# A planned TensorE order, searched on with new costs for scores, V and landings, on one Trainium2 core

## The chip, the cores and the metric

The kernel runs as one program on one core of a Trainium2 chip. The metric is the device time of that core in microseconds (us), the median of several runs. Engines are named as the profile names them: PE is TensorE's matmul and PEld its weight load, DVE is VectorE, ACT is ScalarE, POOL is GpSimd, SP is SyncE, whose queue issues most of the DMAs.

## The reference, cut to what matters

```python
# x: (1, 2048, 576) bf16; 32 heads of 128; 8 memory rows; segments of 32 rows; FFN of 4608
def _A_ref(x, mem0, Wq, Wk, Wv, Wo, seg_len):
    ...
    for s in range(n_seg):                       # 64 segments, one after the other
        h = concatenate([mem, x[segment s]])     # 8 + 32 rows
        q, k, v = h @ Wq, h @ Wk, h @ Wv         # per head
        scores = (q @ k.T) * Dh ** -0.5          # masked with -1e9
        o = softmax(scores) @ v @ Wo
        mem = o[:, :M]                           # the next segment's memory
        outs.append(o[:, M:])
def _B_ref(x, w1, w3, w2):
    return (silu(x @ w1) * (x @ w3)) @ w2
x = x + _A_ref(_layernorm(x), ...)
x = x + _B_ref(_layernorm(x), ...)
x = x + _A_ref(_layernorm(x), ...)               # the same weights
x = x + _B_ref(_layernorm(x), ...)
```

Each layer of attention is a recurrence over 64 segments: a segment's memory rows come out of the segment before.

## The kernel before, in words

The two layers run interleaved, the second LAG = 8 segments behind the first, so a *step* t does segment t of the first layer and segment t - 8 of the second. There are 72 steps; in the first eight and the last eight only one layer is at work (40 columns a product instead of 80). The FFN works on groups of four segments (128 rows), so four steps make a period.

`make_nodes` lists the work as nodes: an engine, a planned duration, dependencies, buffers that it takes (`acq`) and frees (`rel`), and a function that emits the instructions. `plan` turns them into one order for each engine. TensorE's order is not chosen there: it is written out as strings of letters, FIRST (773 nodes), FOUR (208 nodes, a period of four steps, taken eleven times: the *rounds*) and LAST (664 nodes). For the other engines `plan` takes, among the nodes that are ready first by its own costs, the one with the lowest `prio`, so their order, the choice of ACT or VectorE for nodes of kind "AD", the buffer numbers and the order of SP's DMAs follow from the planned costs and from TensorE's letters. The emitter then records the instructions in that order, and each engine runs its own in line.

The letters that the prediction speaks of: Q and q are the products for query and key of four heads (32, and 8 of the weights' last 64 rows); S the scores of a group of eight heads; T transposes of the probabilities on TensorE, in steps of one layer (32 groups in FIRST, 32 in LAST); P the product of the transposed probabilities with V; O and o the output projection (32 and 8); V, v, X, x and G, g the products for V; F and f the FFN's first matmuls for 256 hidden columns, W and w its second for the first and the second layer; a, b, n layer-norm transposes, p the transposes that bring the attention's result back to rows, m those of the memory.

In steps of both layers the probabilities PB (a head group) are transposed into PTS by a DMA that SP issues (`ptd`, L1050); the chain for one group is S on TensorE, add, maximum and subtraction on VectorE, the exponential on ACT, sum, reciprocal and PB on VectorE, the DMA transpose, P. In the plan this DMA is a node "TRD" of `TRD` us with `TRL` us until it has landed. The FFN's weights come in tiles of 256 hidden columns with two buffers each for w1/w3 ("W13": four DMAs) and w2 ("W2l"), all on SP's queue.

The planned costs: `MORE` adds a time by engine and node name, and a change of TensorE's tile form adds SWITCH:

```python
        dur += MORE.get(e, {}).get(n.name, 0.0)
        if e == "PE":
            at += 1
            if not any(m in mode for m in n.mode):
                dur += SWITCH
                settle()
                mode = n.mode
            mode = [m for m in mode if m in n.mode]
```

A node of mode "full/col" can be emitted whole (128 columns of weights) or as two halves of 64 columns; `settle` gives it the form of its neighbours. "row" products work on 64 rows. The emitter's `qk`, when a pair's Q comes ahead of its q in step 0 and the pair is the first or fifth, puts twelve products on the identity in front of it:

```python
            for c in range(4 if first and t == 0 and u % 4 == 0 else 0):
                for _ in range(3):
                    self.mm(self.bk(b[1])[:], self.T.ident[:, 0:P], self.T.W[:, 4 + c, u * 512:(u + 1) * 512], True, True)
```

All matmuls stand under one line of the emitter (L627), all of ACT under L630, all of VectorE under L633, SP's loads under L636.

Of the kernel before, what the change touches and what calls it, by code (L numbers as in the profile page):

```python
# [32 lines left out]
LATS = {"PE": 0.205, "ACT": 0.165, "DVE": 0.14, "POOL": 0.04}  # L33
MORE = {"ACT": {"VMe": 0.13, "VXe": 0.13, "VGe": 0.13, "Yodd": 0.145, "PTe": 0.03, "Fwr": 0.1, "QKe": 0.02, "exp": 0.03},
        "DVE": {"VMe": 0.2, "VXe": 0.2, "VGe": 0.2, "mul": 0.07, "sum": 0.05, "add": 0.03, "POSTa": 0.12, "Fnorm": 0.13, "maxsub": 0.02},
        "PE": {"SC": 0.05, "WOt": 0.03, "VG": 0.03, "FFt": 0.01, "TR": 0.01, "QK": 0.007}}
NOW = 1.0e18
DMA_GROUPS = 4
TRD, TRL = 1.3, 2.3
POOLS = {"bank": 8, "qkt": 4, "sme": 2, "pb0": 1, "pb1": 1, "pts": 2, "ot": 3,  # L40
         "xr": 3, "xn": 2, "w13": 2, "w2": 2, "htt": 3}

# [157 lines left out]
def ewh(*ns):  # L200
# [2 lines left out]


FIRST = (
    "maqqQqQSqTQQQSqQqqSQTQqSXxVvPPTTOOPoPOooOoQqqqqQQSQVvSqqQQQTQSqqXTSPOPTPOOTooPoxOoQQqqqqQSQvVqSQqQQQSqqTPSTOPoOT"
    "PTOPooOoaQqqQQSQqqVvSqQQQqqqTSQPxTSOPXOToToPPOOooQqqqpQQSVvqqQQnQSFfqqQTQSPfqFSOTFPfWoTOPFTOPoofOoFfqqQQWSFQQqqf"
    "vVqQSTFqfQWQQSqfqFPFTSXfPWTOPOxoTFoPOOffooFVqqvQQWQSQqqfFQqqfFSQTWSPQqfqFQFSTOfPWoTOPFTOPfaOoooFfqqQQvqqSQQWSfVF"
    "qQqQWQTQPqSqTOPbSOxxXTXTPooPOOooQpQQqqqqQSnQSFfqFfQvqVSfFWQqqQfPSFPOOooFfPWOFPofOoFQqqfqQWQSqqqQQQSFSGfgqQQqgfFP"
    "GSWPGfggfFFGOPoOOPWOoooFFffqqQQWSqqQQFvSqfVqQQfFSWqQQqfPPSFFOOPWoOffFPoaoOoWQqqqqQQbSQQQqqSGSgqQQqgPGSOPGggGoPOO"  # L210
    "PooOoQqqqppQQQqvVSSnnQFfqqQQQfqqSFFSPfPwOOWoFPoffFOwPWOooFqqffQQwFWQQqqFSSFffqqQQQQqqwWSSgfGFPGgggGPGOoPOOPWOooo"
    "wFqfqqQQQQSffqqFFSQQwvqVWSFQqqffFQWPwSFffPOPOOowooWFPFOoafQQqqqWSQqqqQQQSwSbQqQgqGSggGPGPOGoPgOPOOooo"
)
FOUR = (
    "QqqqppQvVSQQnnQFqfqFSfqqQQFfqQSWPwPSFffOOowFPWoOPFOooFqfqfQQwQQqqgSWGSFqqfQQQPwQSWFqffqFSGgggGPGPOOwooOPWOooFFqq"
    "ffQQQQSwVvqqfFSQQqqWPFSFfqqfQQwOSWPFFoffPOOWPwOoooFfqqQQqqaSQQqWSQQqqqQQSbwSggGGPGPOggoGPOPOOooo"
)
LAST = (
    "QqqppQQSQqqqvVSQQnqqnQSFPqffQOoSPFOFPwWOFPfooOofQQQqqqfFSwWQQFfqqfFSwWqqQQSGqffgFQFPGgWSwPFggfGOOPoGowPOOooFvfqq"
    "VQQQQSWqqFSFqqffQQQQqqSPwWSFfPOOoWwFffPFPOOooowQWQfqqqFSFfqqQQQWSqqqQQSQbvVVSPwXvxPOPOoOPooOoQQppVqqqQQSqvqnQSnQ"  # L220
    "qffFFQTSqqQTPwFfSPWTOOPFffTFooOPWwOooFffqvVQWFQQqqqQSwSQQfqqFSTFfqqQQWTPwSPFOTOffoPTFoPOOWoowxvXVqqQQFSQqfqqQQSF"
    "QQqqqfQTwPSTSWOPFOffTFPToWoPOwOooFqqfvQQQSQqqfVwWSFFfQqqQTWqSPQQqTOSPbOxooTXPTwPOOooQQpqqqQSqQVvnSqqQQqQSQFfqTFP"
    "STfOPoTOwPTFPOOooofVvqqQQQqqSQQSFfqqFQQSTwqqQTFPffSPOTOwxXooPTFPOOffooFQQqqqqQSQFSfvVqqQQQTqqSQwTPfSOFPFTOwTooPf"
    "POfOooFvVQQqwQqqqSQqqQSQfFTSqQqQfPTSPOOooFTTPPfOOoopwfFFnFwffFFwffFFwwffFfFwFfFwffFfFwFfFwffFFwffFFwffFw"
)
ORDER = FIRST + FOUR * 11 + LAST

# [8 lines left out]
def make_nodes(em, nseg, pools, o=Opt, dma_bw=230e3, load_bw=400e3):  # L236
# [125 lines left out]
    def step(t):  # L362
        ls = layers_of(t)
        nl = 2 if both(t) else 1
# [16 lines left out]
        for g in range(NG):  # L381
            qs, qe = [], []
            for u in (2 * g, 2 * g + 1):
                q = Slot("qkt", users=1)
                b = banks()
                pq = t + o.qk + o.ustep * u
                m_ = node("PE", 32 * mm80, em.qk(t, u, b), deps=hx + hm[:1] + ([ld_h[u // 4]] if t == 0 else []),
                          prio=pq, mode="full", acq=[q] + b, name="QK")
                n = node("PE", 4 * mm80, em.qk_tail(t, u, b), deps=hx + hm + ([ld_h[u // 4]] if t == 0 else []), prio=pq + o.qkt, mode="row",
                         acq=[q] + b, name="QKt")  # L390
                rd += [m_, n]
                me[f"QK{u}"], me[f"QKt{u}"] = m_, n
# [7 lines left out]
            sc = node("PE", 8 * (0.0312 if nl == 2 else 0.029), em.scores(t, g, qs, s), deps=qe, prio=pf + o.sc, mode="col" if nl == 2 else "full/col", acq=[s, sme], rel=qs, name="SC")  # L400
# [24 lines left out]
            b = banks()  # L425
            ot = Slot("ot")
            pv = node("PE", 8 * mm80, em.pv(t, g, pts, b), deps=pe_ + vx_ev["VM", t, g] + vx_ev["VX", t - e, g],
                      prio=pf + o.pv, mode="full/col", acq=b + [ot], rel=[pts], name="PV")
            pvs[t, g] = pv
            if paired(t):  # L430
                vx_ev["VX", t + 1, g] = vg_out(t, g, gb, gd + [pv], 0)
            ote = [node("AD", ew(4 * c80), em.ot_ev(t, g, ab, b[ab], ot), deps=[pv], prio=pf, rel=[b[ab]], name="OTe") for ab in (0, 1)]
            wo = node("PE", 32 * mm80, em.wo(t, g, ot), deps=ote + ([ld_o[g]] if t == 0 else []), prio=t + o.wo + o.wog * g, mode="full",
                      acq=[y] if g == 0 else [], name="WO")
            wot = node("PE", 4 * mm80, em.wo_tail(t, g, ot), deps=[wo], prio=t + o.wo + o.wog * g, mode="col", rel=[ot], name="WOt")
            if g:
# [33 lines left out]
    def job(j):  # L470
# [36 lines left out]
        for at, pp in enumerate([npp - 1] + list(range(npp - 1)) if last else range(split, npp)):  # L507
# [5 lines left out]
            for pr_ in (2 * pp, 2 * pp + 1):  # L513
                prio = s0 + o.ff + (o.win if s0 + 4 < nst else o.last_win) * (2 * at + pr_ % 2) / NPR
                if stays:
                    w13, w2 = kept[pr_]
                    ld = []
                    w2s.append(w2)
                elif last:
                    w13 = w2 = None  # L520
                    ld = tail[pp]
                else:
                    keep = s0 < nst <= s0 + 4 and pp == npp - 1
                    w13, w2 = Slot("w13", users=2 + keep), Slot("w2", users=ne + keep)
                    kept[pr_] = w13, w2
                    ld = [node("DMA", kb(1152, 256) / dma_bw, em.load_w13(pr_, w13), prio=prio - 1, acq=[w13], lat=2.5, name="W13")]
                    lds.append(node("DMA", kb(256, 576) / dma_bw, em.load_w2(pr_, w2), prio=prio - 0.99, acq=[w2], lat=2.4, name="W2l"))
                    w2s.append(w2)
                b = banks()
                htt = Slot("htt", users=ne)  # L530
# [862 lines left out]
```

## Time and profile before

| | |
|---|---|
| median of 3 runs | 2644.31 us |
| lowest, highest | 2639.14, 2650.45 us |
| the profiled execution: time, span | 2638.71, 2636.9 us |
| instructions, matmuls | 134690, 60031 |
| busy: PE, DVE, ACT | 98%, 76%, 48% of the span |
| chain that ended last | PE 91%, DVE 4%, DMA 3% |
| mean granted TensorE clock | 0.996 |

The profile is of one execution. A matmul's duration in it is modelled and overlaps the next one's, so the time of a group of products is read from its start to the start of what follows; idle time in brackets names what ended it. One round of FOUR lasts a little over 152 us.

### The profile page before, as it was taken

Reading aid. Unit: us, or ns where it says so; the run is one execution under the profiler, and the core shown is the slowest. Engines: PE = TensorE matmul, PEld = TensorE weight load, DVE = VectorE, ACT = ScalarE, POOL = GpSimd, SP = SyncE. Lnnn points to the kernel's source line nnn. Section 1 sums busy time; section 2 is a strip of 40 time slices with the busy share of each in tenths; the row PEclk is TensorE's granted clock in tenths of the full one; section 3 lists DMA queues with packets and bytes.
Section 4 is the critical chain, followed back from the end, with each engine's and each line's share of the span. In section 5 each row is a group of like instructions: output and inputs, shape, how many; then the busy total and the mean of one; then the engine's idle time right before and its main releaser. Section 6 shows DMA issues by size and latency. Waiting matters only on the chain.

```text
span 2636.9 us, 134690 instructions
## 1 busy us (share of the span) xinstructions
PE 2574.1 (98%) x60031; PEld 2222.3 (84%) x60031; DVE 2004.5 (76%) x5137; ACT 1264.2 (48%) x3745; POOL 196.7 (7%) x253
## 2 busy tenths in 40 slices
PE   5999999999999999999999999999999999999998
PEld 4788888889888888888888888888888888888886
DVE  4787777887778678777877777787777777777876
ACT  2655553444445454444545444454545445454552
POOL 1100000000000010000001001000100001010000
PEclk9999999999999999999999999999999999999999
DMA  9065755575464656546454654655465464545357
GB/s 324 4 174 135 190 104 147 130 148 139 126 147 115 139 127 155 136 131 151 113 140 116 159 140 128 155 110 139 114 156 143 132 159 94 139 122 146 106 156 247
DMA packets 683207, 371.56 MB, mean 141 GB/s; under 512 B 233753, under 2 KB 672801, under 8 KB 681985
## 3 DMA queue, kind: packets, MB, share of 16 engines
q1 hardware_dynamic: 678944, 355.00, 53.2%
q8 instruction: 469, 7.68, 1.2%
q0 software_dynamic: 3024, 6.93, 0.9%
q10 hardware_dynamic: 656, 1.02, 0.2%
q14 instruction: 114, 0.93, 0.1%
HBM read 306.72 MB, written 2.36 MB: 117 GB/s over the span
## 4 chain that ended last, share of the span: by engine, by line
PE 91%; DVE 4%; DMA 3%; issue 1%; ACT 1%; ACTq 0%; DVEq 0%; SPq 0%
PE bank L627 91%; DMA PTS<-PB 2%; DVE HTT L633 1%; DVE PB L633 1%; DVE STAT L633 1%; DMA WV<-in_A_Wv_dram 0%; DVE SME L633 0%; DMA W<-in_A_Wk_dram 0%; DVE V L633 0%; DVE QKT L633 0%; DMA W2C<-in_B_w_dram 0%; DVE XR L633 0%; ACT HTT L630 0%; ACT HT L630 0%; DVE LNS L633 0%
## 5 line engine op out<-in xcount | busy, mean ns | idle before, releaser
L627 PEld LDWEIGHTS <-W 128*128 128x128 bf16 (+2 forms) x32920 | 1261.8, 101 | 119.8 <-issue 67.8
L627 PE MATMUL bank<-HT,W 128*128 128x80 bf16 (+3 forms) x23040 | 795.2, 197 | 21.3 <-ACT HT L630 8.2
L627 PE MATMUL bank<-XTB,W 128*64 128x256 bf16 (+5 forms) x9880 | 658.4, 264 | 2.1 <-issue 1.3
L630 ACT ACTIVATE QKT<-bank 128x256 bf16<-128x256 f32 (+4 forms) x1676 | 385.1, 309 | 302.9 <-PE bank L627 296.5
L627 PE MATMUL bank<-OT,WO 128*128 128x80 bf16 (+3 forms) x11520 | 411.6, 198 | 2.5 <-issue 1.9
L627 PEld LDWEIGHTS <-WO 128*128 128x128 bf16 (+1 forms) x11520 | 383.2, 102 | 29.9 <-issue 16.3
L630 ACT ACTIVATE V<-bank 64x512 bf16<-64x512 f32 (+1 forms) x603 | 338.0, 584 | 137.4 <-PE bank L627 131.4
L627 PE MATMUL bank<-WV,HT 128*32 128x512 bf16 (+4 forms) x3576 | 363.5, 384 | 0.3 <-issue 0.2
L627 PE MATMUL bank<-W2C,HTT 128*64 128x288 bf16 (+1 forms) x3440 | 323.8, 287 | 0.5 <-DMA W2C<-in_B_w_dram 0.5
L630 ACT ACTIVATE HTT<-bank 128x512 bf16<-128x512 f32 (+1 forms) x322 | 172.6, 551 | 300.1 <-PE bank L627 299.1
L633 DVE TENSOR_REDUCE STAT<-SME 104x8 f32<-104x320 f32 (+1 forms) x576 | 274.9, 477 | 28.2 <-ACT SME L630 21.2
L633 DVE TENSOR_TENSOR PB<-SME,STAT 40x128 bf16<-40x128 f32 (+4 forms) x912 | 274.8, 335 | 9.3 <-DMA PTS<-PB 0.5
L627 PEld LDWEIGHTS <-HT 128*32 128x32 bf16 (+4 forms) x3576 | 149.2, 99 | 147.7 <-issue 37.8
L633 DVE SCALAR_TENSOR_TENSOR HTT<-HTT,bank 128x512 bf16<-128x512 bf16 (+1 forms) x322 | 201.0, 624 | 94.4 <-ACT HTT L630 91.6
L627 PEld LDWEIGHTS <-HTT 128*64 128x64 bf16 (+1 forms) x3512 | 233.1, 106 | 31.2 <-DVE HTT L633 4.1
L1047 POOL MEMSET PB<- 128x1024 bf16 x142 | 135.0, 952 | 1657.0 <-DMA PTS<-PB 1114.3
L633 DVE SCALAR_TENSOR_TENSOR XR<-bank,XR 128x288 f32<-128x288 f32 x574 | 240.0, 447 | 20.3 <-PE bank L627 17.2
L630 ACT ACTIVATE OT<-bank 128x320 bf16<-128x320 f32 (+1 forms) x383 | 144.4, 404 | 214.5 <-PE bank L627 185.3
L630 ACT ACTIVATE SME<-SME 104x320 f32<-104x320 f32 (+1 forms) x288 | 135.5, 470 | 194.3 <-DVE SME L633 192.4
L633 DVE TENSOR_TENSOR HTT<-HTT,bank 128x512 bf16<-128x512 bf16 (+1 forms) x322 | 203.3, 631 | 28.5 <-PE bank L627 1.4
L633 DVE CAST V<-bank 64x512 bf16<-64x512 f32 (+1 forms) x261 | 178.9, 686 | 40.1 <-PE bank L627 34.9
L633 DVE TENSOR_TENSOR SME<-bank,maskb 104x320 f32<-104x320 f32 (+1 forms) x288 | 138.5, 482 | 53.8 <-PE bank L627 50.1
(59 smaller groups left out, 1383.5 us busy)
## 6 DMA issues: line engine op xcount, KB each, us to landing
W<-in_B_w_dram SPq DMA_DIRECT2D x608, 256.0 KB, 3.6
W2C<-in_B_w_dram SPq DMA_DIRECT2D x304, 288.0 KB, 3.4
W<-in_B_w_dram SPq DMA_DIRECT2D x608, 32.0 KB, 3.4
W<-in_B_w_dram SPq DMA_DIRECT2D x8, 1024.0 KB, 12.6
W<-in_A_Wq_dram SPq DMA_DIRECT2D x9, 512.0 KB, 9.9
WO<-in_A_Wo_dram SPq DMA_DIRECT2D x4, 1152.0 KB, 19.1
XR<-in_A_x_dram POOLq DMA_DIRECT2D x16, 288.0 KB, 3.1
WV<-in_B_w_dram SPq DMA_DIRECT2D x4, 1152.0 KB, 7.5
```

What stands on the lines that cost most here:

```text
L627: self.ch("PE", self.nc.tensor.matmul(out, lhsT=lhsT, rhs=rhs, start=start, stop=stop, skip_group_check=True, **k))
L630: self.ch("ACT", self.nc.scalar.activation(*a, **k))
L633: self.ch("DVE", getattr(self.nc.vector, fn_)(*a, **k))
L1047: return lambda n: self.ch("POOL", self.nc.gpsimd.memset(self.pbt(pb), 0.0))
```

## The change

Four planned costs of scores and V change: the extra for "SC" on TensorE (0.05 to 0), for "VG" (0.03 to 0.003), for "WOt" (0.03 to 0.022), and the score product itself (0.0312 to 0.0305 with both layers, 0.029 to 0.038 with one). The time to landing becomes 0.2 us shorter for the transposed P and for both kinds of FFN weights. The letters of FIRST, FOUR and LAST are the result of a search that went on from the old ones with these costs. Each string has the same letters as before, in another order; the instructions and data are otherwise the same.

```diff
-        "PE": {"SC": 0.05, "WOt": 0.03, "VG": 0.03, "FFt": 0.01, "TR": 0.01, "QK": 0.007}}
+        "PE": {"SC": 0.0, "WOt": 0.022, "VG": 0.003, "FFt": 0.01, "TR": 0.01, "QK": 0.007}}
...
-TRD, TRL = 1.3, 2.3
+TRD, TRL = 1.3, 2.1
...
 FIRST = (
-    "maqqQqQSqTQQQSqQqqSQTQqSXxVvPPTTOOPoPOooOoQqqqqQQSQVvSqqQQQTQSqqXTSPOPTPOOTooPoxOoQQqqqqQSQvVqSQqQQQSqqTPSTOPoOT"
+    "amQqQqqQqSTQQQqSqqqQSQSTXxVvPPTTOoPPOOooOoQQqqqqQSQQSqvVqQqqTSQPQOSToXPTOPTOPoxoOoQQqqqqQSQvVQSqqQqqQQSSTTPPOaOT"
...
 FOUR = (
-    "QqqqppQvVSQQnnQFqfqFSfqqQQFfqQSWPwPSFffOOowFPWoOPFOooFqfqfQQwQQqqgSWGSFqqfQQQPwQSWFqffqFSGgggGPGPOOwooOPWOooFFqq"
-    "ffQQQQSwVvqqfFSQQqqWPFSFfqqfQQwOSWPFFoffPOOWPwOoooFfqqQQqqaSQQqWSQQqqqQQSbwSggGGPGPOggoGPOPOOooo"
+    "QqqqppQVSvQQnnQfqqFSFqfqQQQfqSFSwPWPOFoffOFPWwOPFOoooFqqffQQQQqqWSwGSFfqgqQQWPQQSwFffqqFGSgggGPGPOOowOPWOoooFFqq"
+    "ffQQQQSWVvfqqFSQQqqwPFSFqqffQQwOSWPoFFPffOOwPWOoooFfqqQQqqaSQQqqWSQQqqQQSbwSggGGPGPOoggGPOPOOooo"
...
-            sc = node("PE", 8 * (0.0312 if nl == 2 else 0.029), em.scores(t, g, qs, s), ...
+            sc = node("PE", 8 * (0.0305 if nl == 2 else 0.038), em.scores(t, g, qs, s), ...
...
-                    ld = [node("DMA", kb(1152, 256) / dma_bw, em.load_w13(pr_, w13), prio=prio - 1, acq=[w13], lat=2.5, name="W13")]
-                    lds.append(node("DMA", kb(256, 576) / dma_bw, em.load_w2(pr_, w2), prio=prio - 0.99, acq=[w2], lat=2.4, name="W2l"))
+                    ld = [node("DMA", kb(1152, 256) / dma_bw, em.load_w13(pr_, w13), prio=prio - 1, acq=[w13], lat=2.3, name="W13")]
+                    lds.append(node("DMA", kb(256, 576) / dma_bw, em.load_w2(pr_, w2), prio=prio - 0.99, acq=[w2], lat=2.2, name="W2l"))
```

More of the change, by code (lines that the diff above doesn't have):

```diff
@@ L205 @@
 FIRST = (
-    "maqqQqQSqTQQQSqQqqSQTQqSXxVvPPTTOOPoPOooOoQqqqqQQSQVvSqqQQQTQSqqXTSPOPTPOOTooPoxOoQQqqqqQSQvVqSQqQQQSqqTPSTOPoOT"
[L207 to L210, printed above, removed]
@@ L211 @@
-    "PooOoQqqqppQQQqvVSSnnQFfqqQQQfqqSFFSPfPwOOWoFPoffFOwPWOooFqqffQQwFWQQqqFSSFffqqQQQQqqwWSSgfGFPGgggGPGOoPOOPWOooo"
-    "wFqfqqQQQQSffqqFFSQQwvqVWSFQqqffFQWPwSFffPOPOOowooWFPFOoafQQqqqWSQqqqQQQSwSbQqQgqGSggGPGPOGoPgOPOOooo"
+    "amQqQqqQqSTQQQqSqqqQSQSTXxVvPPTTOoPPOOooOoQQqqqqQSQQSqvVqQqqTSQPQOSToXPTOPTOPoxoOoQQqqqqQSQvVQSqqQqqQQSSTTPPOaOT"
+    "oTPoPOOooQQqqqVvSQQqqQSQQqQqSTqPSxTXOPoTTOPPoOOooQqqpQQSQqqvVSnQqfFqqQQTSFqfTPQFOSfToPWOPfFTOPFOooofWQQqqqqQSQQS"
+    "FFffqvVqqqQQQWTTSSFPffxXFPWOoTOPTFPOOoooffFQWQqqqqQQSFSfqVvfFQQqqWSQQFfqfTFSTPWPTOOoPofFTOPFOooWQqqfQQSQqqVvSFfQ"
@@ L213 @@
+    "qQqaWqqTQTPSQObSPoXXTTxxPOPOOoooQpqqqQQqSQvqnQfSFVfFqQQqfSFQPWqfSPFFOfOoPWoOofPFOoFfqqQQQQqqWSFSfqqQQqgqGSQQFPfg"
+    "GWSfFPOGgfgFGoPOOPWOoooFFqfqfQQWSqqQQvFSqfVQQqqWSQFqfQfPaSFPOoOPoWOffFPFOooWQQqqqqQSQQbQqqSGSqgqQQPgGSOoPGggGPOO"
+    "PooOoQqqqppQQQSvqqVnnQQSFqffFQQSqqfFSwPWPOOFffFooPwPOWOFooFqqffQQWQQwqqfFSFSqfqQwQQWGSqgqQFPfSGgggGPGOPoOOPwOWoo"
+    "oFFqfqfQQQQqqfSWFVvwSFFqffqQQQQSqqWwPFSffPOOooFPwOWPFOooafQQqqWqSqqQQQQSqwbSQgqqQGSggGPGPOGPgoOPOOooo"
 )
 FOUR = (
-    "QqqqppQvVSQQnnQFqfqFSfqqQQFfqQSWPwPSFffOOowFPWoOPFOooFqfqfQQwQQqqgSWGSFqqfQQQPwQSWFqffqFSGgggGPGPOOwooOPWOooFFqq"
@@ L216 @@
-    "ffQQQQSwVvqqfFSQQqqWPFSFfqqfQQwOSWPFFoffPOOWPwOoooFfqqQQqqaSQQqWSQQqqqQQSbwSggGGPGPOggoGPOPOOooo"
+    "QqqqppQVSvQQnnQfqqFSFqfqQQQfqSFSwPWPOFoffOFPWwOPFOoooFqqffQQQQqqWSwGSFfqgqQQWPQQSwFffqqFGSgggGPGPOOowOPWOoooFFqq"
+    "ffQQQQSWVvfqqFSQQqqwPFSFqqffQQwOSWPoFFPffOOwPWOoooFfqqQQqqaSQQqqWSQQqqQQSbwSggGGPGPOoggGPOPOOooo"
 )
 LAST = (
-    "QqqppQQSQqqqvVSQQnqqnQSFPqffQOoSPFOFPwWOFPfooOofQQQqqqfFSwWQQFfqqfFSwWqqQQSGqffgFQFPGgWSwPFggfGOOPoGowPOOooFvfqq"
-    "VQQQQSWqqFSFqqffQQQQqqSPwWSFfPOOoWwFffPFPOOooowQWQfqqqFSFfqqQQQWSqqqQQSQbvVVSPwXvxPOPOoOPooOoQQppVqqqQQSqvqnQSnQ"
@@ L221 @@
[L221 to L224, printed above, removed]
+    "QqqqppQQQvSqVnSnqqQQQFSfqqQPFOSPofFOPwWOFPfooOofQQqqWwSFfqfFQQQQqfqqFWwGSSFffgqQFPGQWgqwOSoPFggfGGPOFPOOoooWwfqQ"
@@ new lines @@
+    "QQQvqqqVSSFqffQFQQQqqqwSWSPFPfOFOwWoPffFPOOoooWQQqqFSwfqfFQQqqWSQQQqqqQSVSbvVPwOPxvXoPOOPooOoQqqvppQVqqQSQQqqnnQ"
+    "SFfqfqQQTSFSPTFPwOWTffoFPTOPOOoooWwFfqqfQQFSQvVqqqQQSQTWFqfqqQQSwSTPFffFOPwWoFTTffFPOPOOoowoXxvQQqqVqqQSQWSFqqfq"
+    "QQQTSwqfQPFTSTOPWOFffoPTFOPWOooowVvfqqFQQQqqfSwQWSFFfqqqQQTWTSQPqPQOSwbOTXPxooTOPoOoQqqqpQQSQVqvQSqqQqnSQqTfQfPT"
+    "SFPOOTFPooTOPwOfooFVvfqqQQFqqQSQFSwQqqfQQTSfqqFPQOTSXwPToxfOPTFPOOoooFfqqQQqqQSQQFSQfqqvVSwQQqqFTTSPPfFTOOfoPoTw"
+    "POOooFfvVqqqQQwSQqQqfqQSFQQqqfSQTSTPPOOFToTPfPOOooopwfFFnFwffFFwffFFwwffFfFwFffFwFfFwffFFwffFfFwFfFwffFw"
@@ L399, in step @@
             pf = t + o.gstep * g
-            sc = node("PE", 8 * (0.0312 if nl == 2 else 0.029), em.scores(t, g, qs, s), deps=qe, prio=pf + o.sc, mode="col" if nl == 2 else "full/col", acq=[s, sme], rel=qs, name="SC")
+            sc = node("PE", 8 * (0.0305 if nl == 2 else 0.038), em.scores(t, g, qs, s), deps=qe, prio=pf + o.sc, mode="col" if nl == 2 else "full/col", acq=[s, sme], rel=qs, name="SC")
             a = node("DVE", dve(320), em.sm_add(t, g, s, sme), deps=[sc], prio=pf, rel=[s], name="add")
```

## The prediction

> **What bounds the kernel now.** I read the page first, then the busy times by stage, then TensorE's waits, then the timeline of a few places. TensorE is busy nearly all the time:
>
> ```profile
> PE 2574.1 (98%) x60031; PEld 2222.3 (84%) x60031; DVE 2004.5 (76%) x5137; ACT 1264.2 (48%) x3745; POOL 196.7 (7%) x253
> ```
>
> The stages are those of the letter strings: loading, the rest of FIRST, the eleven rounds of FOUR (one round alone, then six), LAST and its tail. The columns are the stretch, its length, each engine's busy time with its instructions, granted clock, DMA share, GB/s:
>
> ```profile
> core 0: us, PE busy (x) PEld busy (x) DVE busy (x) ACT busy (x) POOL busy (x), PEclk, DMA share, GB/s
> 0.00:52.40 52.40, 23.44 (x482) 16.23 (x483) 24.98 (x60) 12.25 (x30) 5.69 (x17) 0.97 1.00 357
> 52.40:522.50 470.10, 457.68 (x11923) 391.54 (x11924) 361.57 (x966) 241.07 (x719) 39.43 (x48) 0.99 0.52 130
> 1134.04:1286.34 152.30, 151.96 (x3408) 132.62 (x3408) 116.82 (x298) 73.84 (x222) 11.20 (x14) 1.00 0.52 136
> 1286.34:2203.30 916.96, 913.43 (x20448) 796.08 (x20448) 702.23 (x1788) 443.00 (x1327) 67.19 (x84) 1.00 0.55 135
> 2203.30:2534.00 330.70, 327.64 (x8020) 279.68 (x8021) 260.46 (x656) 161.69 (x464) 24.64 (x30) 1.00 0.49 127
> 2534.00:2637.00 103.00, 90.83 (x2127) 75.81 (x2121) 70.18 (x179) 37.13 (x104) 3.84 (x5) 0.98 0.71 217
> ```
>
> A round takes 152.30 us with 0.34 us of it idle, and the six later rounds take 916.96 / 6 = 152.83 on average. Eleven rounds therefore hold about 11 x 0.53 = 5.8 us that an order of the same work could still save over the best round. TensorE idles 29.0 us while the weights come in, 12.4 in the rest of FIRST, 3.1 and 12.2 in LAST. Those are all the places where an order can win.
>
> TensorE's waits, first over the eleven rounds (total us, times, longest), then one row of the same view over LAST:
>
> ```profile
> PE bank L627 <- ACT HT L630: 3.8, 11, 0.3
> PE bank L627 <- DMA PTS<-PB: 1.6, 6, 0.3
> ...
> PE bank L627 <- DMA PTS<-PB: 1.8, 2, 1.4
> ```
>
> The first is the hand-over at the end of each round: the next step's Q needs the memory rows that ACT writes after the last o. Both orders end the round in "OPOOooo" and begin the next with Q, so it stays. What is left in the rounds is waiting for P, TensorE's transposed probabilities, to land.
>
> **The change, part by part.** The edited numbers are the planner's costs and enter the kernel only through the built order and the choice of ACT or VectorE for an eviction. What counts is the order.
>
> *Changes of tile form.* TensorE pays when the form of its tile changes (128*128, 128*64, 64*128):
>
> ```profile
> 1451.12 0.32 PE L627 MATMUL bank<-HT,W 64*128 64x80 bf16 x8
> 1451.27 0.38 PE L627 MATMUL bank<-XTB,W 64*128 64x256 bf16 x4
> 1451.49 0.31 PE L627 MATMUL bank<-HT,W 64*128 64x80 bf16 x8
> 1451.73 1.94 PE L627 MATMUL bank<-XTB,W 128*64 128x256 bf16 x32
> ```
>
> Eight products of a q take 0.15 us from start to start when the form stays (1451.12 to 1451.27) and 0.24 when it changes behind them (1451.49 to 1451.73): 0.09 us a change. In the built programs neighbouring products differ in form 1365 times before and 1357 times after: FIRST 347 to 357, each round 66 to 65, LAST 292 to 285. That is -8 x 0.09 = **-0.7 us**. The planner itself counts 1269 to 1250, because it holds a single layer's score products for full form, while the built ones are 64 columns wide; by its count the gain would be 1.7.
>
> *Halved products.* The program has 59,670 products instead of 60,031, because fewer F, G and P are emitted as two halves. A halved F and a whole one cost the same:
>
> ```profile
> 1469.71 1.91 PE L627 MATMUL bank<-XTB,W 128*64 128x256 bf16 x32
> 1474.89 1.91 PE L627 MATMUL bank<-XTB,W 128*128 128x256 bf16 x16
> ```
>
> So this is **0**.
>
> *The start.* FIRST now begins with the layer norm's transposes, the memory's, and then Q of pair 0 ahead of its q. Q first means that twelve products on the identity, which warm the array, are issued for pair 0 too. They read the four chunks of Wk as they land, in line with TensorE's queue:
>
> ```profile
> 23.37 2.44 PE L627 MATMUL bank<-HT,W 128*128 128x40 bf16 x65 [3.16 <-DMA W<-in_A_Wk_dram]
> 30.05 0.45 PE L627 MATMUL bank<-ident,PB 104*128 104x40 bf16 x8 [3.19 <-DVE PB L633]
> 32.47 2.89 PE L627 MATMUL bank<-W,ident 128*128 128x512 bf16 x12
> 35.20 0.96 PE L627 MATMUL bank<-HT,W 128*128 128x40 bf16 x32
> ```
>
> Twelve take 2.73 us (32.47 to 35.20), 0.23 each. Nine fall into the waits for the first three chunks; three follow the last chunk, which TensorE got at 23.37: 0.7 us. Behind it now also come eight products of Q0 and both q (24 products at 2.44 / 65 = 0.038: 0.9), which before ran in the dead time. Some of these 1.6 us return in the 3.19 us wait for PB that follows. Bounds: 0, if that wait swallows it, to +2.7; I take **+1.3**, near the rows that come before the wait. The profile grants a clock of 0.97 over this stage.
>
> The Trainium skill ("TensorE: Matmul & The Clock Gate", Part 1) says that the array runs at half rate until it has been busy for a window of some 3.4 us. By that rule the twelve would let the 65 products behind them run up to twice as fast, an estimate of 1.2 us back, and the start would be +0.1.
>
> *Where P is due in a round.* The strings move S against P. The tightest that moved is the fourth head group of a round's second step. Before (step 37):
>
> ```profile
> 1351.42 0.19 PE L627 MATMUL bank<-QKT 128*64 128x40 bf16 x1
> 1353.05 0.69 DVE L633 TENSOR_TENSOR HTT<-HTT,bank 128x512 bf16<-128x512 bf16 x1
> 1356.06 1.89 PE L627 MATMUL bank<-WV,HT 128*128 128x512 bf16 x8
> 1356.64 0.69 DVE L633 CAST V<-bank 64x512 bf16<-64x512 f32 x1
> 1357.79 0.45 PE L627 MATMUL bank<-PTS,V 128*128 128x80 bf16 x8
> 1358.07 2.46 PE L627 MATMUL bank<-OT,WO 128*128 128x80 bf16 x64
> 1358.49 1.24 SPq L1050 DMA_TRANSPOSE PTS<-PB  x1
> 1360.36 1.15 PE L627 MATMUL bank<-W2C,HTT 128*128 128x288 bf16 x8
> 1361.44 1.73 PE L627 MATMUL bank<-OT,WO 128*64 128x80 bf16 x48
> 1363.01 0.45 PE L627 MATMUL bank<-PTS,V 128*128 128x80 bf16 x8
> ```
>
> The scores end at 1351.61, the transpose is issued at 1358.49 (6.9 later), and TensorE takes P at 1363.01, 11.4 after the scores. The same place in step 25 waited:
>
> ```profile
> 900.19 1.24 SPq L1050 DMA_TRANSPOSE PTS<-PB  x1
> 905.09 0.45 PE L627 MATMUL bank<-PTS,V 128*128 128x80 bf16 x8 [0.22 <-DMA PTS<-PB]
> ```
>
> so its landing took 4.9 us, and the place allows 4.5. After, one G (1.73, from 1356.06 to 1357.79) and one o (eight products, 0.15) no longer lie between S and P: 9.5 us. On VectorE two multiplications for the FFN (0.69 each) leave the chain, so the issue comes some 5.5 us after the scores and 4.0 us are left for landing. Over all transposes:
>
> ```profile
> DMA to landing us min/median/max: 2.6/3.3/6.0
> ```
>
> The half microsecond lost sits between the median, which passes, and the 4.9 of step 25, which would be 0.9 late. I take about 0.14 a round: **+1.5 us**; bounds 0 and 11 x 0.9 = 10.
>
> The place that gains is the fourth group of a round's first step:
>
> ```profile
> 1474.61 0.45 PE L627 MATMUL bank<-PTS,V 128*128 128x80 bf16 x8 [0.32 <-DMA PTS<-PB]
> ```
>
> Between S and P there now lie two more W (0.99 each, 1.08 from 1360.36 to 1361.44 less a change of form), two more P (0.28, from 1357.79 to 1358.07), and one o less: 2.4 us more. The 0.32 shown goes here; of the six waits' 1.6 us I put two thirds to this place: **-1.0**, bounds 0 and -1.6.
>
> *P in the two ends.* In LAST the longest wait of all is the fourth group of the last paired step:
>
> ```profile
> 2346.07 2.59 PE L627 MATMUL bank<-WV,HT 128*32 128x512 bf16 x44
> ...
> 2354.52 0.45 PE L627 MATMUL bank<-PTS,V 128*128 128x80 bf16 x8 [1.37 <-DMA PTS<-PB]
> ```
>
> There V and v (40 products at 2.52 / 44 = 0.057: 2.3 us) move between its S and its P, so the 1.4 goes. Against it, two groups of step 60 come 1.4 us nearer to their S; I take **-0.8** in all. In FIRST the S to P distances, priced as above, shrink: nine of 32 lie under 10 us instead of seven, the shortest 8.0 instead of 8.3. That follows from the shorter landing time in the planner (3.4 us in all instead of 3.6, still above the median of 3.3). **+1.0**, bounds -1 and +3.
>
> Sum: -0.7 + 1.3 + 1.5 - 1.0 - 0.8 + 1.0 = **+1.3 us**. The profiled execution of before took 2638.7 us (2636.9 of span), so its like would take 2640.0. It is 5.6 below the median of the three runs, 2644.3; on that median the forecast is **2645.6 us**.
>
> **The rivals.** *Slower: landings decide.* The planner now gives weights and P 0.2 us less, and the place shown (second step, fourth group) has 4.0 us for landing. If landing there takes 5.2 us or more, TensorE stands over 1.2 us in each of eleven rounds: 13.2 us, 2658 and beyond, with the maximum of 6.0 seen 22 us (2666). It decides above a landing of 4.0. For it: step 25's 4.9, and weight loads that share the DMA engines (0.55 busy). Against: the median of 3.3. The Trainium skill ("DMA: Bandwidth & Descriptors", "Latency and other measured facts") speaks for it: it gives an HBM access 0.2 us on average and 2 us at high load; the spread from 2.6 to 6.0 agrees with that sort of variation, though a P is not read from HBM. Chance 0.14.
>
> *Faster: the ends fill.* If the searched order takes half of the 12.4 and 15.3 us of idle time in FIRST and LAST and all 5.8 of the rounds, that is 13.9 + 5.8 = 19.7, so 2625. For it: the 1.4 us wait that goes. Against: the recurrence at the ends and the loads stay, and the distances in FIRST shrink. Chance 0.10.
>
> *Nothing but tile forms.* Every wait is as before, -0.7: 2643.6. It lies inside the forecast's own case.
>
> **How the numbers follow.** 0.5% is 13 us, about what a measurement of this kernel can tell from no change. The forecast's case, with all its bounds but the two rivals, stays within it: 0.76 for the same, 0.10 faster, 0.14 slower. Low: the median less the 5.8 of the rounds and half of LAST's idle time (7.6), 2631, moved to 2632 by the start. High: the place shown at step 25's 4.9 us (+10) and FIRST at its bound (+3) over 2644.3, 2657. The three runs themselves lie 5 below and 6 above their median, which these ends contain.
>
> **What would show it.** Right: rounds of 152.2 to 153.0 us; the wait for PTS in the rounds at 1 to 4 us, most of it in the second step's fourth group; no wait of 1.4 in LAST; the first products on PB some 2 us later than 30.05, a pair of Q more done before them. Wrong: rounds above 154 us, waits for weights in them, or ends that are 5 us shorter or longer.

## The result and the profile after

The changed kernel takes 2634.29 us (median of 12 runs, 2632.24 to 2638.38) beside 2640.55 for the kernel before (12 runs, 2636.38 to 2650.45): a ratio of 0.9972 [0.9963, 0.998]. Run again in another session it took 2634.09 beside 2642.39: 0.9967 [0.9954, 0.998]. So the change is faster by 6 to 8 us, 0.3%, where +1.3 us was forecast. That lies within the bound of 0.5%, but the measurement resolves it, and its sign is the other one.

The profiled execution took 2636.17 us (span 2634.4). Its busy times on the page are those of before but for a few evictions that went from VectorE to ACT:

```profile
PE 2575.8 (98%) x59670; PEld 2222.5 (84%) x59670; DVE 2005.6 (76%) x5125; ACT 1271.2 (48%) x3757; POOL 197.5 (7%) x253
```

I cut the span at the same events in every trace: the ends of steps 0, 7, 15 and 59, each taken as the start of ACT's last eviction of a step (YTS from a bank, 64 rows). Busy times by these stages, before and after (columns as in the prediction: stretch, length, busy time of each engine, clock, DMA share, GB/s):

```profile
0.00:59.00 59.00, 29.72 (x687) 22.31 (x688) 27.65 (x65) 14.70 (x38) 8.20 (x20) 0.94 0.99 350
59.00:237.50 178.50, 169.34 (x5118) 143.48 (x5118) 137.14 (x379) 98.57 (x282) 16.01 (x19) 0.97 0.35 100
237.50:522.50 285.00, 282.06 (x6601) 241.98 (x6601) 221.76 (x581) 140.06 (x429) 20.91 (x26) 1.00 0.62 145
522.50:2203.30 1680.80, 1674.53 (x37488) 1459.09 (x37488) 1287.30 (x3278) 812.10 (x2432) 123.15 (x154) 1.00 0.56 135
2203.30:2636.90 433.60, 418.47 (x10139) 355.48 (x10138) 330.64 (x834) 198.82 (x567) 28.48 (x34) 1.00 0.54 149
```
```profile
0.00:58.50 58.50, 34.16 (x706) 22.83 (x707) 27.70 (x66) 14.58 (x36) 8.20 (x20) 0.88 1.01 355
58.50:233.40 174.90, 167.43 (x5033) 141.70 (x5033) 135.78 (x380) 98.28 (x281) 15.84 (x19) 1.00 0.35 101
233.40:523.30 289.90, 283.63 (x6585) 243.28 (x6585) 219.08 (x581) 141.23 (x430) 20.84 (x26) 0.99 0.60 142
523.30:2202.00 1678.70, 1673.11 (x37312) 1459.16 (x37312) 1293.57 (x3256) 818.35 (x2453) 124.55 (x154) 1.00 0.57 136
2202.00:2634.40 432.40, 417.46 (x10034) 355.50 (x10033) 329.49 (x842) 198.73 (x560) 28.05 (x34) 0.99 0.52 149
```

In this pair steps 1 to 7 are 3.6 us shorter, steps 8 to 15 4.9 longer, the rounds 2.1 shorter. The pair explains 2.5 us, not 6, and one execution of a kernel differs from another by as much. The experiments gave more traces in which a whole stage has the planned order of before or of after on every engine, so each stage can be averaged over several executions (number in brackets):

| stage | order of before (mean, number) | order of after | difference |
|---|---|---|---|
| step 0 | 59.4 (6) | 58.2 (6) | -1.2 |
| steps 1 to 7 | 177.6 (6) | 174.0 (7) | -3.6 |
| steps 8 to 15 | 286.0 (6) | 288.0 (7) | +2.0 |
| eleven rounds | 1683.6 (5: 1680.8 to 1686.9) | 1679.6 (8: 1678.2 to 1683.2) | -4.0 |
| LAST and tail | 433.8 (6: 432.9 to 435.4) | 434.8 (8: 432.4 to 438.3) | +1.0 |

The sum is -5.8 us, close to what the medians show. The profiled execution of before, from which the prediction was worked out, had the fastest rounds of the five.

### The profile page after: what moved, and what is told of

Its sections match the earlier page's. It is cut to its first block, busy times and chain, and to the rows that moved or that the text cites. A ratio compares the mean times of both kernels' runs of the same rounds, so it can differ in the third digit from the quotient of the medians.

```text
span 2634.4 us, 133901 instructions
## 1 busy us (share of the span) xinstructions
PE 2575.8 (98%) x59670; PEld 2222.5 (84%) x59670; DVE 2005.6 (76%) x5125; ACT 1271.2 (48%) x3757; POOL 197.5 (7%) x253
## 4 chain that ended last, share of the span: by engine, by line
PE 93%; DMA 3%; DVE 3%; ACT 1%; issue 1%; SPq 0%; ACTq 0%; DVEq 0%
PE bank L627 93%; DMA PTS<-PB 2%; DVE HTT L633 1%; DVE STAT L633 1%; DVE SME L633 0%; DVE PB L633 0%; DMA XN<-in_A_x_dram 0%; DVE V L633 0%; DMA W<-in_A_Wk_dram 0%; DMA W<-in_B_w_dram 0%; ACT V L630 0%; ACT HT L630 0%; ACT QKT L630 0%; DVE XR L633 0%; ACT HTT L630 0%
## 5 line engine op out<-in xcount | busy, mean ns | idle before, releaser
L630 ACT ACTIVATE QKT<-bank 128x192 bf16<-128x192 f32 (+4 forms) x1680 | 381.9, 311 | 264.8 <-PE bank L627 260.6
L627 PEld LDWEIGHTS <-WO 128*128 128x128 bf16 (+1 forms) x11520 | 382.1, 102 | 27.6 <-issue 15.2
L630 ACT ACTIVATE V<-bank 32x512 bf16<-32x512 f32 (+1 forms) x577 | 327.5, 585 | 132.3 <-PE bank L627 124.0
L630 ACT ACTIVATE OT<-bank 128x320 bf16<-128x320 f32 (+1 forms) x408 | 153.0, 407 | 251.9 <-PE bank L627 216.0
L633 DVE CAST V<-bank 64x512 bf16<-64x512 f32 (+1 forms) x287 | 196.8, 686 | 42.6 <-PE bank L627 35.9
## 6 DMA issues: line engine op xcount, KB each, us to landing
W2C<-in_B_w_dram SPq DMA_DIRECT2D x304, 288.0 KB, 3.4
XR<-in_A_x_dram POOLq DMA_DIRECT2D x16, 288.0 KB, 2.9
```

What stands on the lines that cost most here:

```text
L627: self.ch("PE", self.nc.tensor.matmul(out, lhsT=lhsT, rhs=rhs, start=start, stop=stop, skip_group_check=True, **k))
L630: self.ch("ACT", self.nc.scalar.activation(*a, **k))
L633: self.ch("DVE", getattr(self.nc.vector, fn_)(*a, **k))
```

## The experiments

Nothing is left out of the computation in any of them; they differ in letters, planned costs or warm-up products.

**Costs and letters apart.** First, which of the two carries the gain. Each edit is a mix of the two kernels:

```diff
 e1_costs:   costs of after;  FIRST, FOUR, LAST of before
 e2_strings: costs of before; FIRST, FOUR, LAST of after
 e3_rounds:  costs of after;  FOUR of after, FIRST and LAST of before
 e4_first:   costs of after;  FIRST of after, FOUR and LAST of before
```

> The new planned costs with the old letters of FIRST, FOUR and LAST: TensorE's nodes run in the old order, only ACT, VectorE, SP and the buffer numbers are planned anew. Theory A (TensorE's order makes the gain): within 2 us of the kernel before. Theory B (the costs make it, through the choice of ACT or VectorE and the order of SP's queue): 4 to 7 us faster.

> The new letters with the old planned costs. Theory A (TensorE's order makes the gain): 4 to 7 us faster than the kernel before, as the whole change. Theory B (the costs make it): within 2 us of the kernel before.

> New costs, new FOUR, old FIRST and LAST. If the rounds make the gain (fewer changes of tile form, fewer waits for P, eleven times): 4 us faster or more, rounds 0.4 us shorter. If the ends make it: 1 to 2 us faster, from the eleven changes of form (1.0) and what is left of the waits for P; rounds near 152.6.

> New costs, new FIRST, old FOUR and LAST. If the first steps make the gain: 3 to 5 us faster, and the first round begins that much earlier. If the rounds make it: within 2 us of the kernel before. By the prediction's own terms it would be 3 us slower (start +1.3, form changes +0.9, P +1.0).

Measured, all beside 2636.29 for before: e1 2707.34 us, 1.0273 [1.0258, 1.0288]; e2 2655.75, 1.0083 [1.0068, 1.0098]; e3 2652.48, 1.0066 [1.0052, 1.0079]; e4 2690.79, 1.0207 [1.019, 1.0224]. Every mix is slower than both kernels, so neither theory held. In e3 the rounds themselves are as short as in the changed kernel (1678.7 us for the eleven); what it loses, it loses under the old FIRST and LAST (steps 1 to 7 take 183.4, LAST 440.1). The new costs alone, on TensorE's old letters, lose 4.2 us a round (e1: 1729.8 us for the eleven beside 1683.6 in the table). TensorE's waits over e1's rounds (total us, times, longest) show on what:

```profile
PE bank L627 <- DMA PTS<-PB: 20.4, 14, 2.5
PE bank L627 <- DVE XN L633: 12.3, 11, 1.1
PE bank L627 <- DVE OT L633: 7.5, 11, 0.7
```

Eleven waits for VectorE's XN and eleven for its OT: one each in every round. e4, whose rounds have the same letters and costs, shows the same two rows (12.3 and 7.5 us in its last step of a round). The planned order of VectorE and ACT differs from that of before in some 27 nodes a round, and SP's DMAs in two. TensorE's letters do not fit that order. The prediction had said that the costs enter only through the built order, and then priced TensorE's order and, at one place, VectorE's.

**Which costs.** The changed kernel with half of its cost changes taken back:

```diff
 e14_oldlandings:  TRD, TRL = 1.3, 2.3; W13 lat=2.5; W2l lat=2.4    (SC, VG, WOt as in after)
 e15_newlandings:  "SC": 0.05, "WOt": 0.03, "VG": 0.03; 0.0312/0.029 (landings as in after)
```

> The changed kernel with the old times to landing (P 2.3, weights 2.5 and 2.4), the other new costs kept. If the landing times are what the new letters are fitted to, it loses most of the 20 us that the new letters lose with all costs old; if the scores and V costs are, it stays within 3 us of the changed kernel.

> The changed kernel with the old costs of scores, V and WOt, the new times to landing kept: the other half of the pair. If the landing times are what the new letters are fitted to, it stays within 3 us of the changed kernel; if the scores and V costs are, it loses most of the 20 us.

e14 took 2637.92 us, 0.9979 [0.9969, 0.9988] beside 2643.36 for before; e15 2661.28, 1.0067 [1.0051, 1.0082]. The times to landing decide next to nothing: without them 13 nodes on VectorE and three DMAs stand elsewhere, none of them in the rounds. The costs of scores and V decide. With the old ones, SP's queue in the first step of a round takes the transpose of a P ahead of two weight loads, and the loads come later. SP's queue in the eighth round of e15 (which begins at 1609.2), then TensorE where that load is used, then TensorE's wait for weights over all its rounds:

```profile
1622.02 1.22 SPq L1050 DMA_TRANSPOSE PTS<-PB  x1
1623.35 7.32 SPq L636 DMA_DIRECT2D W<-in_B_w_dram  x8
```
```profile
1628.92 0.28 PE L627 MATMUL bank<-XTB,W 64*128 64x256 bf16 x1 [0.71 <-DMA W<-in_B_w_dram]
```
```profile
PE bank L627 <- DMA W<-in_B_w_dram: 7.7, 9, 1.4
```

In the changed kernel the same round begins at 1592.8 and both loads go ahead of the P:

```profile
1605.22 5.00 SPq L636 DMA_DIRECT2D W<-in_B_w_dram  x8
1610.32 3.61 SPq L1050 DMA_TRANSPOSE PTS<-PB  x2
```

So the eight DMAs start 12.4 us into the round instead of 14.1, and f does not wait at this place (0.2 us of waits for weights over all the rounds). TensorE's order is the same in both kernels, so these 7.5 us come with the order of SP's queue. The rest of e15's loss, in FIRST and in the rounds, was not followed.

**Which string.** Here each part takes its own costs along, so that every other part keeps the planned order of before on each engine:

```diff
 e16_four:          before; FOUR of after, its costs for the rounds
 e17_first:         before; FIRST of after, its costs for FIRST
 e18_last:          before; LAST of after, its costs for LAST
 e13_before_early:  before; letters of steps 0 to 7 of after, costs of before
 e12_best:          after;  steps 8 to 15 of before, costs of before for FIRST
 e21_oldfirst:      after;  FIRST and its costs of before
```

> The changed kernel with the old letters of FIRST from its step 8 on and, for all of FIRST, the old planned costs; the new letters of steps 0 to 7, FOUR and LAST stay, the last two with the new costs. Theory (the gain of the change sits in steps 0 to 7, and its FIRST loses some 4 us again in steps 8 to 15): steps 0 to 7 in 232 to 235 us, steps 8 to 15 in 284.5 instead of 288 to 290, rounds and LAST as in the changed kernel, so some 3 us under the changed kernel (about 2631). Rival (each string is fitted to the costs and to the string next to it): the borders cost more than is won, and it is no faster than the changed kernel (2634 or more).

> The kernel before with nothing but the letters of steps 0 to 7 new; costs old. Theory (those letters carry the gain, whatever the costs): steps 0 to 7 in about 234 us instead of 237.5, all else as before, so 3 to 4 us faster than before. Rival (the gain there needs the new costs, or is lost in steps 8 to 15, which inherit another state of buffers and loads): no faster than before, or slower.

> The kernel before with the new letters of FOUR alone; the new costs are in force for the rounds and the old ones outside, so that FIRST and LAST have the order of before on every engine and the rounds that of the changed kernel. Theory R (the rounds gain, because a P that lands late costs less at the new places; old rounds took 1680.8, 1682.4 and 1686.9 us in three profiled executions, new ones 1678.2 to 1681.0): 4 to 6 us faster than before, and the scatter of its runs as narrow as that of the changed kernel. Theory F (the gain sits in steps 0 to 7): no faster than 2 us.

> The kernel before with the new letters of FIRST alone, with the new costs for FIRST: FIRST as in the changed kernel on every engine, the rest as before. Theory F: steps 0 to 7 shorter by 4 to 6 us, steps 8 to 15 longer by 4, and in all the 6 to 8 us of the whole change, or most of it. Theory R: 0 to 2 us faster.

> The kernel before with the new letters of LAST alone, with the new costs for LAST. The prediction held this part at -0.8 us (the 1.4 us wait for P that goes) less 0.6 for changes of tile form; the two profiled pairs show -0.7 on average. Expected by both theories: 0 to 2 us faster.

> The changed kernel with FIRST as it was, the old costs in force for it. The new FIRST alone was at +2.4 us with an interval of -0.8 to +5.3, the new rounds at -6.6, the new LAST at -0.5. If these add up, it is 7 us faster than before, so the same as the changed kernel or 1 us better; if the new FIRST does gain beside the new rounds, it is 2 to 3 us slower than the changed kernel.

| kernel | us | before | ratio [95%] |
|---|---|---|---|
| e13_before_early | 2646.67 | 2643.36 | 1.001 [0.9998, 1.0022] |
| e12_best | 2638.51 | 2643.36 | 0.9982 [0.9973, 0.999] |
| e16_four | 2637.54 | 2643.68 | 0.9975 [0.9966, 0.9984] |
| e17_first | 2644.91 | 2643.68 | 1.0009 [0.9997, 1.002] |
| e18_last | 2643.3 | 2643.68 | 0.9998 [0.9987, 1.0009] |
| e21_oldfirst | 2638.26 | 2641.22 | 0.9988 [0.9979, 0.9997] |

The theory that the letters of steps 0 to 7 carry the gain falls with e13, and the best version that it pointed to, e12, is no faster than the changed kernel (0.9982 beside 0.9967 to 0.9972). The rounds carry most: alone they bring 6.6 us of the medians (0.0025 x 2643.7; 4.2 to 9.0). The new LAST brings nothing that these runs resolve. FIRST stays unclear: alone it costs 2.4 us (-0.8 to +5.3), but without it the kernel is 0.9988 and not 0.9967 to 0.9972, so beside the new rounds it seems to bring 4 to 6 (by the intervals, some 1 to 10). Its stages in the traces say -2.8 in all. The first two do not agree within their intervals, and I do not settle on one.

**What in the rounds.** TensorE's waits over the rounds of e13, whose rounds have the order of before, and of e16 (HT and P as in the prediction's fence; W is a tile of w1/w3, W2C one of w2):

```profile
PE bank L627 <- DMA W<-in_B_w_dram: 3.3, 5, 1.3
PE bank L627 <- DMA PTS<-PB: 3.2, 7, 1.0
PE bank L627 <- DMA W2C<-in_B_w_dram: 0.8, 2, 0.5
```
```profile
PE bank L632 <- ACT HT L635: 3.8, 11, 0.3
PE bank L632 <- DMA PTS<-PB: 1.7, 5, 0.6
```

Over the five executions with old rounds TensorE waits 2.0 us for weights (0.5, 0.9, 4.1, 1.8, 2.7) and 2.2 for P; over the eight with new ones 0.04 and 2.5. The weights are late mostly at one place of the first step, at the f that is the first to use a new tile (13 of the 19 waits of the five, 7.3 of their 10.0 us); nearly all others are at the w that follows some 3 us later. In e13's eighth round (beginning at 1597.4), SP and TensorE:

```profile
1617.05 1.26 SPq L1050 DMA_TRANSPOSE PTS<-PB  x1
1618.41 3.86 SPq L636 DMA_DIRECT2D W<-in_B_w_dram  x4
```
```profile
1622.50 2.34 PE L627 MATMUL bank<-XTB,W 128*64 128x256 bf16 x36
1626.13 0.39 PE L627 MATMUL bank<-XTB,W 64*128 64x256 bf16 x3 [1.29 <-DMA W<-in_B_w_dram]
```

The load is issued 21.0 us into the round; over 55 old rounds the last of its four DMAs lands at 25.0 to 28.7, in the median at 26.5. An undisturbed f wants it at 26.3. In the changed kernel's round:

```profile
1614.02 2.28 SPq L636 DMA_DIRECT2D W<-in_B_w_dram  x4
```
```profile
1620.08 0.33 PE L627 MATMUL bank<-OT,WO 128*64 128x80 bf16 x8
1620.34 0.61 PE L627 MATMUL bank<-XTB,W 64*128 64x256 bf16 x8
```

The load is issued at 21.2 and lands at 25.6 to 28.6 (88 rounds, median 26.8), but O and o now stand ahead of the two f, and the second f comes at 27.75. A row of waits stands there in 2 rounds of 88 instead of 13 of 55.

These rows understate a wait, since they count it from the modelled end of the product before and leave out what is under 0.15 us: in e17's first round 0.88 us lie between two starts at this f (26.22 and 27.10), and the row says 0.61. So I also counted from start to start. The eight products of the two f start within 0.34 us of each other when nothing holds them up. With the old order they take longer in 30 rounds of 55, each time with a load that lands no earlier than the second f is due, and lose 3.2 us in eleven rounds on average; with the new order in 5 of 88, and lose 0.3. Counted in a similar way (a product's distance from the start before it, less the lower quartile of that distance at its place over all rounds, where more than 0.08 us are left), w loses 0.8 us to late weights with the old order and nothing with the new, and P 4.3 and 5.3. The shortest round, which nothing disturbs, took 152.30 us with the old order and 152.19 with the new, and 0.09 of the difference is in the first step, as one change of tile form less would make it. That gives -2.9 and -0.8 for weights, +1.0 for P and 11 x -0.11 = -1.2 for the undisturbed round: -3.9 of the -4.0 us that the rounds gain in the traces. All of the gain is in the first step of a round (39.0 to 39.5 us on average in the five old executions, 38.75 to 38.9 in seven of the eight new ones); the other three steps differ by less than 0.1.

**The place alone.** I moved only these letters, once in each kernel:

```diff
 e19_later (before):   -...QSWPwPSFffOOowFP...   +...QSWPwPSFOffOowFP...
 e20_earlier (after):  -...SwPWPOFoffOFPWw...    +...SwPWPFffOoOFPWw...
```

> The kernel before with one letter of FOUR moved: in the first step the two f behind PSF come after the first of the two O (PSFffOO becomes PSFOffO), so that the second f, which is the first to use a new tile of w1/w3, begins at 27.5 instead of 26.3 us into the round; the tile lands at 26.4 in the median. One more change of tile form a round costs 11 x 0.09 = 1.0 us. Theory W (the new rounds gain because this tile no longer comes late): the waits for weights in the rounds fall from 2.0 us to under 0.4, and the time by 0.5 to 1.5 us net. Rival (the waits follow from the load of the DMA engines and not from the place): waits for weights at 1 to 4 us as before, and 1 us slower.

> The changed kernel with the same place put back: in the first step the O and the o ahead of the two f come behind them (POFoffO becomes PFffOoO), so that the second f begins at about 26.3 instead of 27.75 us into the round; as many changes of form. Theory W: the waits for weights in the rounds rise from 0.05 us to 1.5 to 4, and the kernel is slower than the changed one by as much (2636 to 2638 beside 2634). Rival: waits for weights stay under 0.5 and the time within 1 us of the changed kernel.

e19 took 2642.82 us, 1.0005 [0.9994, 1.0016] beside 2641.22; e20 2656.03, 1.0058 [1.0043, 1.0074]. Their waits over the rounds, e19 first:

```profile
PE bank L627 <- DVE HTT L633: 2.2, 8, 0.3
PE bank L627 <- DMA PTS<-PB: 1.4, 5, 0.4
PE bank L627 <- DMA W<-in_B_w_dram: 1.3, 2, 0.7
```
```profile
PE bank L627 <- DMA PTS<-PB: 12.5, 17, 1.5
PE bank L627 <- issue: 5.2, 33, 0.2
PE bank L627 <- ACT HT L630: 4.1, 12, 0.3
PE bank L627 <- DMA W<-in_B_w_dram: 3.5, 5, 1.9
```

In e19 the waits for weights fall less than expected, from 2.0 us to 1.6 (1.3 for W and 0.3 for W2C). The f is late in 2 rounds of 11 instead of 6, with loads that land at 28.4 and 29.0, and loses 1.9 us by its starts instead of 3.2. The later f also makes the w that follows wait for VectorE's HTT in eight rounds: 2.2 us that eat the gain. In e20 the weights are late as expected (from 0.04 to 3.5 us by the rows; by starts the f is late in 8 rounds of 11 and loses 6.8 us). But the kernel loses some 23 us beside the changed one (1.0058 less 0.997) and not 3: with the f earlier, a weight load (26.2 us into the sixth round) goes ahead of a P (28.5) in SP's queue, where the changed kernel has the P at 26.2 and the load at 27.6, and TensorE waits 12.5 us for P instead of 2.5 on average. So the place costs what theory W said, in one profiled execution of each kernel, but in neither could it be moved by itself: both shifts turned into another wait. The rows of "issue" of 0.2 us that some traces show and others of the same kernel do not (33 here, none in the profile after) are products missing from the record (59628 in the second execution of the changed kernel, with such rows, where 59670 weight loads stand), and I left them out of the sums for the rounds.

**Two terms of the prediction.** The twelve warm-up products of pair 0 left out of the changed kernel, and the S of the second step's fourth group put back ahead of its G:

```diff
 e8_nowarm0:  -for c in range(4 if first and t == 0 and u % 4 == 0 else 0):
              +for c in range(4 if first and t == 0 and u == 4 else 0):
 e9_place13:  FOUR  -...qFGSgggGPGPOOowOP...   +...qFSGgggGPGPOOowOP...
```

> The changed kernel without the twelve products on the identity ahead of the first pair's Q; all engines' orders are otherwise the same. By the prediction's term for the start, three of them lie behind the last chunk of Wk: 0.7 us faster, and step 0 ends that much earlier than at 58.0. If they pay by warming the array: step 0 ends 0 to 1.2 us later. If the start has slack ahead of the loads of V: no change at the end of step 0.

> The changed kernel with one letter of FOUR moved back: in the second step of each round the fourth group's S stands ahead of the G again, as before the change, so 1.7 us more lie between S and P. By the prediction's term the place costs 1.5 us over the eleven rounds: 1 to 2 us faster, and no wait for P in front of the fourth group of the steps 17, 21, 25 and on. If the place costs nothing on average: no change. If what the planner makes of the moved letter for VectorE costs more: slower by 3 us or more, the rounds longer by 0.3 us each.

e8 took 2639.49 us, 0.999 [0.998, 1.0]: some 5 us slower than the changed kernel (2634.09 in that session), though its orders are the same. TensorE in the profile after, then in e8's:

```profile
17.35 4.87 PE L627 MATMUL bank<-W,ident 128*128 128x512 bf16 x12 [3.94 <-DMA W<-in_A_Wk_dram]
22.06 3.46 PE L627 MATMUL bank<-HT,W 128*128 128x40 bf16 x128
25.45 0.37 PE L627 MATMUL bank<-QKT 128*40 128x40 bf16 x8
```
```profile
21.30 4.25 PE L627 MATMUL bank<-HT,W 128*128 128x40 bf16 x121 [1.05 <-DMA W<-in_A_Wk_dram]
25.48 0.45 PE L627 MATMUL bank<-QKT 128*40 128x40 bf16 x8
```

The twelve delay the projections by 0.76 us (21.30 to 22.06), and the projections then take 26.5 ns each ((25.45 - 22.06) / 128) instead of 34.5 ((25.48 - 21.30) / 121). The scores start at the same time. In six executions with the twelve the scores start at 25.2 to 26.1, so the term of +0.7 for the twelve is zero within the scatter. Why e8 is 5 us slower in the median is not explained by this place; its step 0 ends 1.0 to 1.5 us later than that of the two executions of the changed kernel, and the rest was not found.

e9 took 2635.47 us, 0.9967 [0.9955, 0.9978], the same as the changed kernel: the place costs nothing either way.

**The two kernels again**, as a yardstick for the traces:

> The changed kernel once more, for a second profile of it beside the kernel before of the same session. If the gain sits in the steps of one layer at the start, the end of step 7 lies 3 to 7 us ahead of the 237.0 us of before again, and the 2.8 us wait for P in step 8 of the first profile need not return. If it sits in the rounds, they are 2 us shorter in all and the first steps differ less than 2 us.

> The kernel before once more, for a second profile. The end of step 7 within 1 us of 237.0, that of step 15 within 3 us of 522.0, eleven rounds within 1.5 us of 1680.8, and from the end of step 59 to the end of the span within 3 us of 434.1, if these are properties of the order and not of one execution.

The changed kernel's second profiled execution took 2634.26 us, that of before 2638.56 (span 2636.8). Step 7 of the changed kernel ends at 231.7, as was expected of a gain in the first steps, but its rounds take 1681.0 us, no less than in the first trace of before. In the second trace of before the rounds take 1682.4, just outside the 1.5 us that were allowed; the other three marks are met. Their stages are in the table of means.

## Why the prediction missed

By its own steps, the forecast was +3.2 for FIRST (start 1.3, P 1.0, forms 0.9), -0.5 for the rounds (forms -1.0, P +1.5 and -1.0) and -1.4 for LAST (P -0.8, forms -0.6). The stages measured -2.8, -4.0 and +1.0. FIRST missed by more than the rounds did, but only for the rounds did a kernel of their own show the gain.

*The rounds: the step that failed* is the sentence "What is left in the rounds is waiting for P". It rests on the rows of one profiled execution, in which a wait for weights came once (0.5 us). In others with the same order these rows come to 4.1 us, and even in that one the second f is late by its starts in four of the eleven rounds, 0.7 us that no row shows. On average late weights cost some 4 us of the old rounds and 0.3 of the new. The prediction then compared distances from S to P and never those from a weight load to the f that uses it first. What stands ahead of it says that SP's queue follows from the planned costs, and it did not price a load that is moved past a P, in either direction. In the rounds the change moves one load ahead of a P and the f 1.4 us later.

*P in the rounds.* The second step's fourth group was to cost 1.5 us and the first step's to gain 1.0. Averaged over the executions, TensorE's waits for P are 0.35 us in the second step before and 0.34 after, 1.6 and 1.8 in the first (counted by starts 1.0 and 1.0, 2.7 and 3.4). The cost in the second step is nothing, and the gain in the first did not come. Nor did the rival that the landings decide (13 us and more): the step with the place that has 4.0 us left for its landing waits no more than before.

*LAST.* The wait of 1.4 us for the fourth group was to go. It did not: it is 1.0 in the profile after and 1.4 again in the second execution, 2.8 us before the end of the last paired step as before; with the old LAST two executions (e13, e16) do without it. The row is that of the second execution over LAST:

```profile
PE bank L627 <- DMA PTS<-PB: 1.4, 1, 1.4
```

Placing V and v between its S and its P did not end the wait, so the distance on TensorE was not what set it; what did was not followed.

*The start.* The row that it was read from was an outlier: the last chunk of Wk came at 23.37 us there, and at 21.2 to 22.0 in the other five executions with the old start. At the place that was priced, the first products on PB, +1.3 is near the mark: 28.5 us on average with the old start and 29.6 with the new (six executions each). That is luck in part: the twelve cost nothing, as e8 shows, and behind the last chunk now come 128 products instead of 65, a Q and a q more than the 24 that were counted, in 3.4 us instead of 2.4. And step 0 ends 1.2 us earlier, not later; what brings that was not followed. The Trainium skill ("TensorE: Matmul & The Clock Gate", Part 1) has the array at half rate until it has been busy for a while. The trace agrees: in the profile after, products of 512 columns start 0.43 us apart on average up to 21.19 and 0.22 at the end, and the trace's first clock record, of 1.00, begins at 21.68. In e8, without the twelve, that record begins at 34.39, and the projections take 34.5 ns each instead of 26.5: they gain a quarter, not the half of the estimate. The granted clock of 0.97 that the prediction read for the loading stage says little about its start: in that trace the first record begins at 32.77, and time without a record counts as full.

*The rest of FIRST* was held at +0.9 for forms and +1.0 for P. Steps 1 to 7 gained 3.6. TensorE's idle time there falls from 8.2 to 6.5 us on average, with the wait for PTS on ACT down from 1.8 to 0.65; the other half of the gain was not followed. With the old costs under the new letters (e2, e12, e13) the stage takes 176.5 us, mostly because VectorE's PB comes late; e13 and then the profile after, over this stage:

```profile
PE bank L627 <- DVE PB L633: 2.5, 3, 1.2
```
```profile
PE bank L627 <- DVE PB L633: 0.8, 2, 0.4
```

So there, too, the letters without the costs that they were searched with bring only 1.1 of the 3.6. In steps 8 to 15 two us go back to weights (0.4 to 1.2 us) and P (1.6 to 2.6 us). That P costs 1.0 more in FIRST was therefore right on average; single executions scatter from 0.3 to 4.1.

*Halved products* at nothing and 0.09 for a change of form fit the undisturbed rounds (152.30 and 152.19 us, with one G and one P fewer in halves and one change of form less); they met no other test. The medians shift by 3.8 us between three runs of before (2644.31) and twelve (2640.55), so a third of the distance from 2645.6 to 2634.3 was the base and not the change.

## What to carry to other kernels

When a planner builds several engines' orders from one list of costs, an order that was searched with it and those costs are one thing: here each half without the other lost 19 to 71 us. Read a change of such costs first from the queue that is filled in order (SP's here): which load passes which transfer, and who is the first to use what it brings. Where the margin between a landing and its use is under the spread of landings (25.0 to 28.7 us beside a use at 26.3), one profiled execution does not show the wait; take several before the terms are sized, and compare starts of products, since a list of idle times hides short waits.

## What the hardware showed that I had not expected

The same order of instructions ran its eleven rounds in 1680.8 to 1686.9 us, with the spread in waits for DMAs. SP took 2.1 to 3.9 us to issue the same four weight DMAs, at the same place of the round. The warm-up products cost their own time and give it back within 3.4 us.

A granted clock of 1.00 at the start can mean that none was recorded. The same twelve products on the identity run in the profile after at 17.35 for pair 0 and at 30.68 for pair 4, about 0.4 us each both times ((35.55 - 30.68) / 12 is 0.41). Their two stretches, where the third value from the right is the clock:

```profile
17.00:22.00 5.00, 4.65 (x12) 1.55 (x12) 0.00 (x0) 0.00 (x0) 0.00 (x0) 1.00 1.05 407
30.00:36.00 6.00, 6.00 (x56) 2.85 (x53) 0.33 (x1) 0.56 (x2) 0.00 (x0) 0.56 1.03 425
```

The second shows a throttle: a record of 0.5 ends at 35.33, and until then the products start 0.43 us apart. In the first the trace has no clock record before 21.68, and the view counts such time as 1.00, but the products start as far apart as in the second, and closer from 21.68 on. That they read chunks of weights that land every 1.3 us is not the reason: the second and third product on a chunk wait for nothing new and still start 0.38 to 0.43 us after the one before. In e4 the first record begins earlier, at 20.14, and there the products behind it start 0.22 us apart and do wait for the chunks:

```profile
20.46 0.81 PE L627 MATMUL bank<-W,ident 128*128 128x512 bf16 x3 [0.65 <-DMA W<-in_A_Wk_dram]
21.71 0.81 PE L627 MATMUL bank<-W,ident 128*128 128x512 bf16 x3 [0.44 <-DMA W<-in_A_Wk_dram]
```

In the second execution of the changed kernel the record of 0.5 ends at 32.90, the stretch from 30 to 36 has 0.76, and pair 4's products are done about a microsecond earlier, at 34.57 instead of 35.55.
